# Eight weight chunks a step, loads ten chunks ahead, and small sums moved between engines in an attention and feed-forward kernel

## The chip, the cores and the metric

The kernel runs on one core of a Trainium2 chip. The metric is the device time of one execution in microseconds (us); where several runs were made, their median. Five engines work beside each other: TensorE (PE, with its weight loads as PEld), VectorE (DVE), ScalarE (ACT), GpSimd (POOL) and SyncE (SP), which issues all DMAs here. Each takes its instructions in the order in which they stand in its own stream, and they wait for each other by semaphores.

## The reference

Attention over 4 batches, 8 heads, 576 tokens and 64 dimensions, in which each query keeps only its 32 highest scores, then two feed-forward layers over the 2304 tokens:

```python
def _attn_ref(q, k, v):
    scores = scale * np.matmul(q, k.transpose(0, 1, 3, 2))
    kth = np.partition(scores, -top_k, axis=-1)[..., -top_k:-top_k + 1]
    mask = scores >= kth
    scores = np.where(mask, scores, -1000000000.0)
    scores = scores - np.max(scores, axis=-1, keepdims=True)
    attn = np.exp(scores)
    attn = attn / (np.sum(attn, axis=-1, keepdims=True) + 1e-09)
    return np.matmul(attn, v)

def _moe_ref(x, w_in, w_out, g_ln):       # 512 -> 1024 -> 512
    h = x @ w_in
    solu = h * softmax(h)
    ln = (solu - mu) / np.sqrt(var + 1e-06) * g_ln
    return ln @ w_out

def _moe2_ref(x, w_in, w_out):            # 512 -> 2048 -> 512
    h = x @ w_in
    g = h * (1.0 / (1.0 + np.exp(-1.702 * h)))
    return g @ w_out
```

(The softmax, the mean and the variance of the second function are shortened here.) Inputs and outputs are 32-bit.

## The kernel before

**Numbers.** Every matrix operand is split into a high and a low 16-bit half, and a product is made of three matmul passes. DVE, ACT and POOL make the halves: ACT writes the high one, POOL (or DVE) the difference. The weights come as 64-bit words: `w_load` brings a chunk of 128 x 1024 words (512 KB) into two slots of the tile `wt`, `w_decode` makes 32-bit numbers of it on DVE (two or three operations of 512 columns, L246 to L251, by way of a tile `wi` in PSUM), and `w_split` makes the two halves with ACT and POOL (L288, L135). There are 48 chunks: eight for w1, eight for w2, and four times four and four for the two matrices of the second layer.

**Attention** runs in 72 steps (18 blocks of queries, four or two steps in each). A step has `scores` (PE, L452), `copy_s` (ACT), `fold` and `rounds` (DVE, L470 to L484: the 32nd highest value by repeated maxima), `pick` (POOL, L494), `mask` (ACT and POOL, L502), `exp_of` (ACT), `high` and `low` (ACT and POOL, L520), `turn` (a transpose by DMA of `eh` into `et`, L525), and three steps later `back` (PE, L603: `av`). When a block's last step is back, `evac_main` or `evac_tail` divides by the sums of the exponentials: `recip` adds 1e-9 to the tile `rsum` and takes the reciprocal (L626, L627), once for each of the 20 blocks of queries (16 of 8 heads, 4 of half as many columns). The addition is two operations, on all columns but the last and on the last.

**Feed-forward** work comes in 18 blocks of 128 tokens, spread over 13 places of the program each, one place per step and two in steps 6 and 7 (`SLOTS`). Within it `c` is L804 (tile `h2`, shown as `h`), `gelu` L813, `g_low` L824 (tile `gh`) and `d` L831 (tile `o`). The buffers `t` and `y` are one pair (tag `t`), and `o` has one buffer, so that the next block's first `d` waits until `store` has made `y` of the last one.

**What sets the order.** The code is written in steps, and a scheduler then orders each engine's stream by its own estimate of times. `DECODE` says how many chunks are decoded in which step, `W_RAW` how many chunks ahead of the one being decoded are loaded, `W_STAGE` how many slots of `wt` must stay free when a load takes its two. After the first k and q tiles, `w_loads(-1)` starts the loads.

**The end.** `w_check` squares all weights on ACT (tile `junk`, sums into `insq`). At the end the sums of squares are added over the partitions (L1117, on POOL), several bounds are tested on DVE (`inside`, L1108 to L1111), the result `bad` is joined over the partitions (L1126, on POOL), and `flag` (L1128) decides on a branch to a second, exact version of the whole program, which does not run in the profiled execution.

Of the kernel before, what the change touches and what calls it, by code (L numbers as in the profile page):

```python
# [7 lines left out]
F32 = mybir.dt.float32  # L8
# [4 lines left out]
ALU = mybir.AluOpType  # L13
# [6 lines left out]
FIRST_RAW = (None, None, "h", "zt", None)  # L20
FIRST_HALF = (False, True, True, False, True)
W_RING = 4
W_RAW = 6
W_STAGE = 4
TWO_BANKS = 32
HP_W = 0
SIGNED = (1, 1, 0)
# [1 line left out]
DELAY = 0  # L29
HP_AT = 0  # L30
LAG = 3
DECODE = (4, 4, 4, 4, 8, 8, 8, 8)
SLOTS = {6: 2, 7: 2}
FIRST_SLOT = 6
R_BUFS = 2
# [5 lines left out]
TAIL_AT = (1,)  # L41
W_CHECK = 60
PIN_TO = -1
KV_BUFS, RAW_BUFS = 4, 2
S_IN = 2.0 ** 8
S_EXP = 2.0 ** -19
S_Z = 2.0 ** 10
# [4 lines left out]
def attn_moe_kernel(tc: tile.TileContext, *args):  # L52

    nc = tc.nc
    with ExitStack() as ctx:
        flag = layers(ctx, tc, True, *args)
        again = nc.values_load(flag, min_val=0, max_val=1)
    with tc.If(again > 0):
        with ExitStack() as ctx:
            layers(ctx, tc, False, *args)  # L60
# [19 lines left out]
def layers(ctx, tc, quick, q, k, v, w1, w2, g_ln, w3, w4, out):  # L80
# [5 lines left out]
    nc = tc.nc  # L86
    start = len(nc.cur_bb.bb.instructions)
# [10 lines left out]
    cst = ctx.enter_context(tc.tile_pool(name="cst", bufs=1))  # L98
# [6 lines left out]
    if quick:  # L105
        picks = cst.tile([128, B * S * H // 128, 3], F32, name="picks")
        pickc = cst.tile([128, 2, 3], F32, name="pickc")
        insq = cst.tile([128, 2 * B * NP + 24], F32, name="insq")
        qsq = cst.tile([128, B * (NEWT + 1)], F32, name="qsq")
        zsq = cst.tile([128, NBLK], F32, name="zsq")  # L110
        ysum = cst.tile([128, NBLK], F32, name="ysum")
        for i, x in enumerate((1.0, -S_EXP, BIG)):
            nc.vector.memset(pickc[:, :, i], x)

    lo_n = {}

# [31 lines left out]
    sm = ctx.enter_context(tc.tile_pool(name="sm", bufs=3))  # L148
    PS = bass.MemoryType.PSUM
    p_sc = ctx.enter_context(tc.tile_pool(name="p_sc", bufs=1, space=PS))  # L150
    p_av = ctx.enter_context(tc.tile_pool(name="p_av", bufs=1, space=PS))
# [43 lines left out]
    def room(i, n, keep):  # L195

        live = {r + z for r in at_raw.values() for z in range(2)}
        free = [r for r in range(i, WCH + SHIFT) if r not in live]
        fit = [r for r in free if all(r + z in free for z in range(n))
               and len(set(free) - {i, r, r + n - 1}) >= keep]  # L200
        if not fit:
            return None
        r = min(fit, key=lambda r: (max(used.get(r + z, -1) for z in range(n)), -r))
        for z in range(n):
            used[r + z] = i
        return r
# [415 lines left out]

    def recip(r, n):

        for a, b in ((0, n - 1), (n - 1, n)):
            nc.vector.tensor_scalar(r[:, a:b], r[:, a:b], 1e-9, None, op0=ALU.add)  # L626
        nc.vector.reciprocal(r, r)  # L627

    def evac_main(blk):
        b, r = blk  # L630
        if r == 0:
            batch_coef(b)
        recip(rsum[blk], 8)
        if quick:
            rr = rsum[blk].rearrange("p (a c) -> p a c", c=2)
        else:
            rr = sm.tile([128, 4, 2], F32, tag="rr", name="rr")
            iv = bsc[b][:, 1, 1, :]
            nc.vector.scalar_tensor_tensor(rr, rsum[blk].rearrange("p (a c) -> p a c", c=2), bcf[b][:, 1:2],
                                           iv[:, :, None].to_broadcast([128, 4, 2]), op0=ALU.mult, op1=ALU.mult)  # L640
        x = one.tile([128, 512], F32, tag="x", name="x")
        nc.vector.tensor_tensor(x.rearrange("p (h d) -> p h d", d=64),
                                pav[blk].rearrange("p (h d) -> p h d", d=64),
                                rr.rearrange("p a c -> p (a c)")[:, :, None].to_broadcast([128, 8, 64]),
                                op=ALU.mult)
        return x, None if quick else bcf[b][:, 2:3]
# [255 lines left out]
    def run(gen):  # L902
        for _ in gen:
            pass
# [49 lines left out]
    def w_loads(i, most=99):  # L954

        while wload[0] < min(WCH, i + 1 + W_RAW, most):
            j = wload[0]
            r = room(j, 2, max(1, min(W_STAGE, (WCH + SHIFT - j - 2) // 2)))
            if r is None:
# [6 lines left out]
    def decode(n):  # L966
        for _ in range(n):
            i = wnext[0]
            if i == WCH:
                return  # L970
            wnext[0] += 1
            with urgent(tc, HP_W):
                w_decode(i)
                w_split(i)
                w_loads(i)
# [47 lines left out]
    def place(name):  # L1023
        for f in slot.get(name, ()):
            with urgent(tc, HP_MOE):
                f()

    t = 0
    while True:
        count = 0 if t < FIRST_SLOT else SLOTS.get(t, 1)  # L1030
        live = t < NS
        for z in range(max(count, 1)):
# [53 lines left out]
            place("late")  # L1086
            if z < count - 1 and t < len(DECODE):
                decode(DECODE[t] // count)
        if live:
            for w in work.get(t, ()):  # L1090
                run(loaded.pop(0))
            if t < len(DECODE):
                decode(DECODE[t] - (DECODE[t] // max(count, 1)) * (max(count, 1) - 1))
        if W_CHECK <= t < W_CHECK + WCH // 2:
# [9 lines left out]
    ok = sm.tile([128, 6], F32, tag="ok", name="ok")  # L1104

    def inside(x, lo, hi, dst):

        nc.vector.tensor_scalar(junkc[:, 0:x.shape[1]], x, lo, None, op0=ALU.is_ge)  # L1108
        nc.vector.scalar_tensor_tensor(junkc[:, 0:x.shape[1]], x, hi, junkc[:, 0:x.shape[1]], op0=ALU.is_le,
                                       op1=ALU.mult)  # L1110
        nc.vector.tensor_reduce(dst, junkc[:, 0:x.shape[1]], axis=AX.X, op=ALU.min)  # L1111
# [1 line left out]
    short = one.tile([128, B * S * H // 128], F32, tag="zt", name="short")  # L1113
    nc.vector.scalar_tensor_tensor(short, picks[:, :, 2], -1.0 / BIG, picks[:, :, 0], op0=ALU.mult, op1=ALU.add)
    junkc = one.tile([128, short.shape[1]], F32, tag="x", name="junkc")
    tot = sm.tile([128, insq.shape[1]], F32, tag="tot", name="tot")
    nc.gpsimd.partition_all_reduce(tot, insq, channels=128, reduce_op=bass_isa.ReduceOp.add)  # L1117
    inside(tot, 4.0, 2.0 ** 15, ok[:, 0:1])
    inside(qsq, 2.0 ** -7, 2.0 ** 14, ok[:, 1:2])
    inside(short, -1e30, 0.0, ok[:, 2:3])  # L1120
    inside(zsq, 2.0 ** -28, 2.0 ** 60, ok[:, 3:4])
    inside(ysum, -1e30, 1e30, ok[:, 4:5])
    nc.vector.tensor_reduce(ok[:, 5:6], ok[:, 0:5], axis=AX.X, op=ALU.min)
    bad = sm.tile([128, 2], F32, tag="bad", name="bad")
    nc.vector.tensor_scalar(bad[:, 0:1], ok[:, 5:6], 0.5, None, op0=ALU.is_lt)
    nc.gpsimd.partition_all_reduce(bad[:, 1:2], bad[:, 0:1], channels=128, reduce_op=bass_isa.ReduceOp.max)  # L1126
    flag = sm.tile([128, 1], I32, tag="flag", name="flag")
    nc.vector.tensor_scalar(flag, bad[:, 1:2], 0.5, None, op0=ALU.is_gt)  # L1128
    return flag[0:1, 0:1]


# [28 lines left out]
```

## Time and profile before

| what | us |
|---|---|
| median of 3 runs | 978.17 (976.66 to 978.33) |
| the profiled execution | 977.06 |
| its span on the core | 975.3 |
| busy: PE, DVE, ACT, POOL | 761.6, 771.0, 721.1, 696.6 |
| granted TensorE clock, mean over the span | 0.929 of full speed |

The profiled execution lies 1.1 us under the median; 1.8 us of it lie outside the span. In the first 30 us the first tiles are loaded and turned. Up to some 260 us weights are loaded and decoded beside attention, until 840 us attention and feed-forward blocks run together, and what is left of the feed-forward blocks follows until 965 us. A row of the timeline gives start, duration, engine, line, operation, tiles (out<-in), shapes and, in brackets, how long the engine was idle before it and what ended that.

### The profile page before, as it was taken

How to read it: one execution, taken by the hardware profiler on the slowest of the kernel's cores; microseconds unless marked ns; L12 is line 12 of the kernel's file. 1: busy time of each engine (PE TensorE's matmuls, PEld its weight loads, DVE VectorE, ACT ScalarE, POOL GpSimd, SP SyncE). 2: the span in 40 equal slices, each digit the busy share in tenths (PEclk: the TensorE clock that was granted, in tenths of full speed). 3: DMA queues.
4: the chain of work that ended last, by engine and by line, in shares of the span. 5: the costliest groups of instructions: out<-in, count | busy, mean ns of one | idle time of the engine just before them, and what ended most of it. 6: DMA issues, size and time to landing. Idle time of an engine off the chain costs nothing.

```text
span 975.3 us, 22249 instructions
## 1 busy us (share of the span) xinstructions
PE 761.6 (78%) x8224; PEld 498.0 (51%) x8224; DVE 771.0 (79%) x2170; ACT 721.1 (74%) x1257; POOL 696.6 (71%) x700
## 2 busy tenths in 40 slices
PE   1123526546779899998979999898989999999975
PEld 0012213424446566665556766566565666666643
DVE  4999899989989889897798989889798899421210
ACT  4788888578888877878887877778887888743421
POOL 1489799688888887787878777687887677722311
PEclk9998667677999999999999999999989999999988
DMA  6998766476786756666856756668767555522100
GB/s 157 314 276 185 195 152 144 92 146 156 153 146 127 148 109 111 115 123 123 161 108 129 140 100 120 107 115 155 141 104 120 104 97 104 91 47 45 34 22 15
DMA packets 337733, 122.66 MB, mean 126 GB/s; under 512 B 315344, under 2 KB 329168, under 8 KB 337616
## 3 DMA queue, kind: packets, MB, share of 16 engines
q1 hardware_dynamic: 337616, 121.16, 60.5%
q8 instruction: 66, 1.08, 0.5%
q14 instruction: 51, 0.42, 0.1%
HBM read 39.85 MB, written 4.72 MB: 46 GB/s over the span
## 4 chain that ended last, share of the span: by engine, by line
POOL 21%; ACT 17%; PE 16%; DVE 15%; DMA 15%; issue 10%; SPq 5%; ACTq 0%; POOLq 0%; DVEq 0%
PE h L804 5%; POOL s L502 5%; PE o L831 5%; ACT s L157 5%; POOL eh L520 4%; DVE wk L481 4%; DVE wk L484 4%; DMA raw<-in_k_dram 3%; PE x L774 3%; POOL gh L824 2%; ACT r L157 2%; POOL e L768 2%; POOL wt L135 2%; POOL kq L135 2%; DMA vraw<-in_v_dram 2%
## 5 line engine op out<-in xcount | busy, mean ns | idle before, releaser
L481 DVE MAX8 wk<-wk 128x8 f32<-128x296 f32 x576 | 239.5, 453 | 0.0
L804 PE MATMUL h<-x2t,wt 128*128 128x128 f16 x3456 | 218.0, 225 | 23.4 <-DVE t L813 14.6
L804 PEld LDWEIGHTS <-wt 128*128 128x128 f16 x3456 | 207.4, 101 | 30.1 <-issue 13.4
L502 POOL TENSOR_TENSOR s<-s,r 128x576 f32<-128x576 f32 x144 | 181.6, 1281 | 43.0 <-ACT r L157 42.8
L520 POOL TENSOR_TENSOR eh<-s,eh 128x576 f16<-128x576 f32 x144 | 181.3, 1280 | 36.9 <-ACT eh L157 27.0
L831 PE MATMUL o<-wt,gh 128*128 128x512 f16 x864 | 201.3, 383 | 7.2 <-ACT y L157 7.1
L484 DVE MATCH_REPLACE8 wk<-wk 128x296 f32<-128x296 f32 x432 | 191.6, 449 | 0.0
L603 PE MATMUL av<-vt,et 128*128 128x64 f16 (+1 forms) x2400 | 90.9, 204 | 83.8 <-DMA et<-eh 78.8
L452 PE MATMUL sc<-kt,qt 128*128 128x64 f16 (+7 forms) x640 | 97.4, 320 | 63.3 <-DVE wk L473 45.6
L824 POOL TENSOR_TENSOR gh<-t,gh 128x512 f16<-128x512 f32 x72 | 83.4, 1159 | 80.5 <-ACT gh L157 73.5
L831 PEld LDWEIGHTS <-gh 128*128 128x128 f16 x864 | 83.9, 99 | 102.9 <-issue 11.3
L603 PEld LDWEIGHTS <-et 128*128 128x128 f16 (+1 forms) x2400 | 83.4, 108 | 97.6 <-DMA et<-eh 86.4
L157 ACT ACTIVATE s<-s,picks 128x576 f32<-128x576 f32 x144 | 110.1, 766 | 14.3 <-POOL s L502 14.0
L813 DVE SCALAR_TENSOR_TENSOR t<-t,h 128x512 f32<-128x512 f32 x72 | 48.6, 675 | 83.5 <-ACT t L157 81.5
L774 PE MATMUL x<-wt,zt 128*128 128x512 f16 x432 | 102.8, 392 | 14.8 <-DMA zt<-zh 13.2
L157 ACT ACTIVATE r<-s,picks 128x576 bf16<-128x576 f32 x144 | 103.2, 764 | 7.6 <-POOL picks L494 7.4
L707 PE MATMUL ha<-wt,xt 128*128 128x512 f16 x432 | 100.6, 391 | 10.3 <-DMA xt<-xhl 9.4
L452 PEld LDWEIGHTS <-qt 128*128 128x128 f16 (+1 forms) x640 | 48.8, 110 | 110.7 <-DVE wk L473 39.4
L157 ACT ACTIVATE s<-sc 128x1152 f32<-128x1152 f32 x72 | 80.4, 1117 | 17.8 <-PE sc L452 9.5
L157 ACT ACTIVATE wt<-wt 128x512 f16<-128x512 f32 (+1 forms) x115 | 68.5, 627 | 26.2 <-DVE wt L251 11.1
L157 ACT ACTIVATE t<-h 128x512 f32<-128x512 f32 x72 | 42.1, 584 | 59.9 <-PE h L804 54.8
L157 ACT ACTIVATE eh<-s 128x1152 f16<-128x1152 f32 x72 | 83.1, 1154 | 0.6
(81 smaller groups left out, 1066.1 us busy)
## 6 DMA issues: line engine op xcount, KB each, us to landing
wt<-in_moe_w_in_dram SPq DMA_DIRECT2D x24, 512.0 KB, 5.1
wt<-in_moe_w_out_dram SPq DMA_DIRECT2D x24, 512.0 KB, 6.1
qt<-qt SPq DMA_DIRECT2D x72, 64.0 KB, 2.0
raw<-in_k_dram SPq DMA_DIRECT2D x32, 128.0 KB, 2.7
raw<-in_q_dram SPq DMA_DIRECT2D x16, 256.0 KB, 3.2
vraw<-in_v_dram SPq DMA_DIRECT2D x32, 128.0 KB, 2.5
out_dram<-y SPq DMA_DIRECT2D x16, 256.0 KB, 2.4
et<-eh SPq DMA_TRANSPOSE x72, 4.7
```

The lines of the kernel that those rows point to most:

```text
L157: nc.scalar.activation(out, in_, func, **kw)
L452: nc.tensor.matmul(sc[rows, i * S + c0:i * S + c1], t[qi // 4][:, hl, qi % 4, rows], kts[kp][:, k0 + c0:k0 + c1], start=(hl == 0), stop=(h ...
L481: nc.vector.max(out=wk[:, i, at_:at_ + 8], in_=wk[:, i, 0:W_END])
L484: nc.vector.match_replace(out=wk[:, i, 0:W_END], in_to_replace=wk[:, i, at_:at_ + 8], in_values=wk[:, i, 0:W_END], imm_value=LOW)
L502: nc.gpsimd.tensor_tensor(s[:, i], s[:, i], r[i], op=ALU.subtract)
L520: nc.gpsimd.tensor_tensor(eh[:, 1, cols], s[:, i], eh[:, 0, cols], op=ALU.subtract)
L603: nc.tensor.matmul(o[rows, col:col + 64], et[:, ea, 4 * i + c, rows], vts[kp][:, va, vc:vc + 64], start=(n == 0), stop=(n == 14))
L707: nc.tensor.matmul(h[:, half * 512:half * 512 + 512], self.xt[:, a, kc], w1v(kc, w, half), start=(n == 0), stop=(n == 11))
L774: nc.tensor.matmul(self.x2, self.zt[:, a, kc], w2v(kc, w), start=(n == 0), stop=(n == 23))
L804: nc.tensor.matmul(h2[:, mm * 128:(mm + 1) * 128], w3v(kc, w, 4 * g + mm), self.x2t[:, a, kc], start=(n == 0), stop=(n == 11))
L824: nc.gpsimd.tensor_tensor(gh[:, 1], t.rearrange("p (a n) -> p a n", a=4), gh[:, 0], op=ALU.subtract)
L831: nc.tensor.matmul(self.o, gh[:, a, mm], w4v(4 * g + mm, w), start=(g == 0 and n == 0), stop=(g == 3 and n == 11))
```

## The change

Four edits:

- `DECODE` is (8, 8, 8, 8, 8, 8) in place of (4, 4, 4, 4, 8, 8, 8, 8), `W_RAW` 10 in place of 6, `W_STAGE` 6 in place of 4. The 48 chunks are asked for in steps 0 to 5 and loads run up to ten chunks ahead. `SLOTS` is as before.
- `recip` adds 1e-9 to all columns in one operation with two tensor inputs, (r + 1e-9) max r, in place of two operations with one.
- The sum of `insq` over the partitions is a matmul with a 128 x 128 tile of ones, into a PSUM tile that has the buffer of `av`, in place of POOL's partition sum.
- The joining of `bad` over the partitions is such a matmul too, of one column, and `flag` is read from PSUM. POOL sets the tile of ones to 1.0 at the start.

```diff
-W_RAW = 6
-W_STAGE = 4
+W_RAW = 10
+W_STAGE = 6
...
-DECODE = (4, 4, 4, 4, 8, 8, 8, 8)
+DECODE = (8, 8, 8, 8, 8, 8)
...
+        ones = cst.tile([128, 128], F32, name="ones")
+        nc.gpsimd.memset(ones, 1.0)
...
     def recip(r, n):
 
-        for a, b in ((0, n - 1), (n - 1, n)):
-            nc.vector.tensor_scalar(r[:, a:b], r[:, a:b], 1e-9, None, op0=ALU.add)
+        nc.vector.scalar_tensor_tensor(r[:, 0:n], r[:, 0:n], 1e-9, r[:, 0:n], op0=ALU.add, op1=ALU.max)
         nc.vector.reciprocal(r, r)
...
-    tot = sm.tile([128, insq.shape[1]], F32, tag="tot", name="tot")
-    nc.gpsimd.partition_all_reduce(tot, insq, channels=128, reduce_op=bass_isa.ReduceOp.add)
+    tot = p_av.tile([128, 512], F32, tag="av", name="tot")[:, 0:insq.shape[1]]
+    nc.tensor.matmul(tot, ones, insq, start=True, stop=True)
...
-    bad = sm.tile([128, 2], F32, tag="bad", name="bad")
-    nc.vector.tensor_scalar(bad[:, 0:1], ok[:, 5:6], 0.5, None, op0=ALU.is_lt)
-    nc.gpsimd.partition_all_reduce(bad[:, 1:2], bad[:, 0:1], channels=128, reduce_op=bass_isa.ReduceOp.max)
+    bad = sm.tile([128, 1], F32, tag="bad", name="bad")
+    nc.vector.tensor_scalar(bad, ok[:, 5:6], 0.5, None, op0=ALU.is_lt)
+    rows = p_av.tile([128, 512], F32, tag="av", name="rows")[:, 0:1]
+    nc.tensor.matmul(rows, ones, bad, start=True, stop=True)
     flag = sm.tile([128, 1], I32, tag="flag", name="flag")
-    nc.vector.tensor_scalar(flag, bad[:, 1:2], 0.5, None, op0=ALU.is_gt)
+    nc.vector.tensor_scalar(flag, rows, 0.5, None, op0=ALU.is_gt)
```

In the built programs the scheduler's order differs as well. Lines after the change are numbered two or three higher. First POOL's stream at the end of the program before, from the low half `gh` of the feed-forward blocks (the numbers tell the buffers of different stages apart; an ISA row is an instruction that belongs to the partition sum or to the change between it and other work):

```order
L824 TENSOR_TENSOR gh_13153<-t_13134,gh_13153 128x512
L1117 ISA
L1117 ISA tot_13463<-insq_75 128x56
L824 ISA
L824 TENSOR_TENSOR gh_13222<-t_13206,gh_13222 128x512
L824 TENSOR_TENSOR gh_13291<-t_13275,gh_13291 128x512
L824 TENSOR_TENSOR gh_13362<-t_13345,gh_13362 128x512
L824 TENSOR_TENSOR gh_13429<-t_13413,gh_13429 128x512
L1126 ISA
L1126 ISA bad_13481<-bad_13481 128x1
```

The same place after the change, from the same `gh` (now buffer 13135) to the load of the flag:

```order
L826 TENSOR_TENSOR gh_13135<-t_13116,gh_13135 128x512
L826 TENSOR_TENSOR gh_13204<-t_13188,gh_13204 128x512
L826 TENSOR_TENSOR gh_13273<-t_13257,gh_13273 128x512
L826 TENSOR_TENSOR gh_13344<-t_13327,gh_13344 128x512
L826 TENSOR_TENSOR gh_13411<-t_13395,gh_13411 128x512
L58 TENSOR_LOAD flag_13467
```

The two sums and the three other ISA rows are gone from POOL. On PE the matmul of `tot` stands behind the 48 `h` matmuls of the stage whose `gh` is 13273, ahead of the `o` matmuls that read `gh` 13204, and the matmul of `rows` is PE's last.

Second, SP's stream near the start, before: transposes of the third and fourth pair of heads' keys (`kt`), chunk loads (`wt`), the tail of q, the first v tiles and the first transposed exponentials (`et`):

```order
L356 DMA_TRANSPOSE kt<-kq 128x10x128
L215 DMA wt<-in_moe_w_in_dram 128x1024 x4
L391 DMA raw<-in_q_dram 64x2x64
L215 DMA wt<-in_moe_w_in_dram 128x1024
L356 DMA_TRANSPOSE kt<-kq 128x10x128
L215 DMA wt<-in_moe_w_in_dram 128x1024
L215 DMA wt<-in_moe_w_out_dram 128x1024 x2
L362 DMA vraw<-in_v_dram 128x256
...
L215 DMA wt<-in_moe_w_out_dram 128x1024 x6
L525 DMA_TRANSPOSE et<-eh 128x18x128
```

The same stretch of SP after the change:

```order
L359 DMA_TRANSPOSE kt<-kq 128x10x128
L218 DMA wt<-in_moe_w_in_dram 128x1024 x6
L218 DMA wt<-in_moe_w_out_dram 128x1024 x2
L394 DMA raw<-in_q_dram 64x2x64
L359 DMA_TRANSPOSE kt<-kq 128x10x128
L218 DMA wt<-in_moe_w_out_dram 128x1024 x6
L218 DMA wt<-in_moe_w_in_dram 128x1024 x2
L365 DMA vraw<-in_v_dram 128x256
...
L528 DMA_TRANSPOSE et<-eh 128x18x128
```

Sixteen chunk loads in place of eight stand ahead of the first v tile, and sixteen in place of fourteen ahead of the first `et`. On DVE the order of the decode differs little: the first 36 chunks' last operations (L251, now L254) stand behind the same number of folds as before, and the 48th stands behind the 17th fold in place of the 19th.

Third, DVE's stream at the second main block of queries, before (the reciprocal of `rsum` and what lies around it):

```order
L473 MAX wk<-sc 128x8 x2
L626 TENSOR_SCALAR rsum<-rsum 128x7
L246 TENSOR_SCALAR wi<-wt 128x512
L626 TENSOR_SCALAR rsum<-rsum 128x1
L481 MAX wk<-wk 128x8 x2
L251 SCALAR_TENSOR_TENSOR wt<-wt,wi 128x512
L627 RECIPROCAL rsum<-rsum 128x8
```

And after the change:

```order
L476 MAX wk<-sc 128x8 x2
L628 SCALAR_TENSOR_TENSOR rsum<-rsum 128x8
L253 SCALAR_TENSOR_TENSOR wi<-wt,wi 128x512
L484 MAX wk<-wk 128x8 x2
L629 RECIPROCAL rsum<-rsum 128x8
```

One operation stands where there were two, at the same place behind the fold's maxima.

## Rows read from the trace of the kernel before

**Rows 1.** The page's busy time, share of the span and instructions of each engine.

```profile
PE 761.6 (78%) x8224; PEld 498.0 (51%) x8224; DVE 771.0 (79%) x2170; ACT 721.1 (74%) x1257; POOL 696.6 (71%) x700
```

**Rows 2.** Busy time in three stretches; last: granted clock, DMA share, GB/s.

```profile
25.00:50.00 25.00, 4.18 (x16) 1.74 (x16) 24.05 (x63) 17.62 (x33) 12.64 (x16) 1.00 1.01 325
25.00:300.00 275.00, 135.62 (x1324) 85.28 (x1325) 259.77 (x675) 220.81 (x386) 228.64 (x226) 0.82 0.75 177
300.00:800.00 500.00, 466.76 (x5316) 309.93 (x5314) 439.50 (x1303) 405.56 (x704) 395.50 (x400) 0.98 0.66 122
```

**Rows 3.** Timeline near the end, 935 to 957 us, the rows around PE's gap.

```profile
935.80 0.62 ACT L157 ACTIVATE gh<-t 128x512 f16<-128x512 f32 x1
936.59 2.84 PE L804 MATMUL h<-x2t,wt 128*128 128x128 f16 x48
936.93 0.68 POOL L1117 PARTITION_ALL_REDUCE tot<-insq  x1 [5.85 <-ACT gh L157]
...
939.53 0.60 ACT L157 ACTIVATE t<-h 128x512 f32<-128x512 f32 x1 [3.12 <-PE h L804]
...
944.59 1.14 POOL L824 TENSOR_TENSOR gh<-t,gh 128x512 f16<-128x512 f32 x1 [6.98 <-issue]
945.76 0.60 ACT L157 ACTIVATE y<-o 128x512 f32<-128x512 f32 x1 [5.63 <-POOL gh L824]
...
946.50 4.65 PE L831 MATMUL o<-wt,gh 128*128 128x512 f16 x12 [7.07 <-ACT y L157]
...
953.67 2.75 PE L831 MATMUL o<-wt,gh 128*128 128x512 f16 x12
```

**Rows 4.** The stretch of those slower matmuls, with columns as in rows 2.

```profile
946.50:951.00 4.50, 4.50 (x13) 1.66 (x13) 0.00 (x0) 0.47 (x1) 1.15 (x1) 0.57 0.15 58
```

**Rows 5.** Timeline of PE behind a shorter wait in the same stage.

```profile
913.00 3.63 PE L774 MATMUL x<-wt,zt 128*128 128x512 f16 x16 [1.58 <-DMA zt<-zh]
```

**Rows 6.** Timeline of the last two instructions.

```profile
968.21 0.38 POOL L1126 PARTITION_ALL_REDUCE bad<-bad  x1 [5.80 <-issue]
968.62 0.15 DVE L1128 TENSOR_SCALAR flag<-bad 128x1 int32<-128x1 f32 x1 [2.55 <-POOL bad L1126]
```

**Rows 7.** DVE's groups by shape: xcount | busy us, mean ns | idle before.

```profile
L626 DVE TENSOR_SCALAR rsum<-rsum 128x7 f32<-128x7 f32 x16 | 15.3, 958 | 4.1 <-ACT s L157 4.1
L250 DVE SCALAR_TENSOR_TENSOR wi<-wt,wi 128x512 int32<-128x512 int32 x21 | 14.3, 681 | 0.0
...
L627 DVE RECIPROCAL rsum<-rsum 128x8 f32<-128x8 f32 x16 | 3.0, 190 | 0.1
...
L626 DVE TENSOR_SCALAR rsum<-rsum 128x1 f32<-128x1 f32 x20 | 2.8, 140 | 4.7 <-ACT s L157 4.7
```

**Rows 8.** Timeline of the longest addition on DVE and of POOL beside it.

```profile
170.36 9.36 DVE L626 TENSOR_SCALAR rsum<-rsum 128x7 f32<-128x7 f32 x1
...
170.27 1.17 POOL L135 TENSOR_TENSOR wt<-wt 128x512 f16<-128x512 f32 x1
...
178.53 1.17 POOL L135 TENSOR_TENSOR wt<-wt 128x512 f16<-128x512 f32 x1
```

**Rows 9.** Timeline of another addition on DVE and of POOL beside it.

```profile
721.45 0.63 DVE L626 TENSOR_SCALAR rsum<-rsum 128x3 f32<-128x3 f32 x1 [0.38 <-ACT s L157]
...
720.89 1.16 POOL L824 TENSOR_TENSOR gh<-t,gh 128x512 f16<-128x512 f32 x1
```

**Rows 10.** Timeline of DVE and POOL near 14 us, and all of L288 (ns min/median/max).

```profile
13.83 0.83 DVE L138 SCALAR_TENSOR_TENSOR kq<-raw,kq 128x640 f16<-128x640 f32 x1 [0.94 <-ACT kq L157]
...
14.40 1.27 POOL L288 TENSOR_TENSOR wt<-wt 128x512 f32<-128x512 f32 x1 [0.92 <-ACT wt L157]
...
L288 POOL TENSOR_TENSOR wt<-wt x27: 1144/1156/1272, 12.3 to 249.2; 128x512 f32<-128x512 f32 x27
```

**Rows 11.** Timeline of ACT: the first v tile, and the fifth step's score copy.

```profile
44.17 0.74 ACT L157 ACTIVATE vraw<-vraw 128x640 f32<-128x640 f32 x1 [0.41 <-DMA vraw<-in_v_dram]
...
64.56 1.10 ACT L157 ACTIVATE s<-sc 128x1152 f32<-128x1152 f32 x1
```

More of the change, by code (lines that the diff above doesn't have):

```diff
@@ L43 @@
 PIN_TO = -1
-KV_BUFS, RAW_BUFS = 4, 2
+KV_BUFS = 4
+RAW_BUFS = 2
 S_IN = 2.0 ** 8
```

## The prediction

> **What bounds the kernel now.** I read the busy shares first, then the windows by stage, then the stretch in which the matmul engine drains, then single lines. No engine is the bound of the whole run: PE 78%, DVE 79%, ACT 74%, POOL 71% of the span [rows 1]. By stage it differs. From 25 to 300 us, where weight chunks are decoded beside attention, DVE is busy 259.8 of 275 us (94%) and PE 136. From 300 to 800 us PE is busy 466.8 of 500 and DVE 439.5 [rows 2]. After some 840 us attention is over, only the feed-forward blocks drain, and PE is their bound. So a microsecond of DVE is worth most before 300 us, and after 840 us each idle stretch of PE is a loss.
>
> Such a stretch is there. PE ends the h matmuls that began at 936.59 at 939.43 (2.84 us) and starts the next o matmul at 946.50: 7.07 us idle. Followed back: o waits for ACT's y (945.76), y for POOL's gh (944.59), because y takes the buffer of t that this gh reads. Its ACT half was ready at 936.42 (935.80 + 0.62), yet POOL began it 6.98 us after the sum over partitions had ended, waiting for nothing that the profile shows [rows 3]. The order of before has a row "ISA" ahead of the sum and another ahead of that gh; I read the 6.98 us as the second one. The idle time costs twice: the granted clock was 0.57 in 946.5 to 951, and the 12 matmuls there took 4.65 us, against 2.75 for the next twelve [rows 3, 4].
>
> **The drain (gain 7.5 us).** The first sum becomes one PE matmul, and POOL runs its gh rows without anything between. This gh can then run at 936.5 and end at 937.7. ACT's order is still t, y, gh, so y starts when t ends, 939.53 + 0.60 = 940.13, and o starts 0.74 us later, as it did before (945.76 to 946.50): 940.87 in place of 946.50, a gain of 5.63 us. PE then idles some 1.4 us in place of 7.1. After the 1.58 us wait at 913.00 sixteen matmuls took 3.63 us, 0.23 each, as in the next twelve (2.75 / 12) [rows 5], so I take the clock as kept: 4.65 - 2.75 = 1.90 us more. What is late next is y behind ACT's t; it leaves the 1.4 us. The new matmul, 56 columns of 32-bit data, is queued on PE just ahead of that o group and waits for ACT's last check of the weights, which stands ahead of the gh of 935.80 on ACT and is over by then. No row shows a 32-bit matmul. Nearest rows: 48 of 128 columns in 2.84 us (0.06 each) and 12 of 512 in 2.75 (0.23 each); as an estimate 0.1 to 1.6 us, from two of the short to seven of the long. Up to 1.4 us it lies inside the idle time and costs nothing; above that it moves o by 0.2. DVE's checks of it stand ahead of one gelu row, whose reader has 2.6 us of o matmuls to spare.
>
> **The last sum (gain 1.9 us).** DVE's flag waited 2.55 us, from the end of bad on DVE to 968.62, and the sum on POOL began 5.80 us after POOL's last gh, not after bad [rows 6]. In its place stands a matmul of one column: 0.1 to 1.6 us by the same rows. I take 0.6, since one column is nearer to the short one: 2.55 - 0.65 = 1.9 us, bounds 0.9 to 2.4. All of it is on the path. The 6.5 us from the flag to the end of the span stay.
>
> **The small additions (gain 1.7 and 4 us).** Each of the 20 calls of recip loses one DVE operation: 20 x 0.140 = 2.8 us [rows 7]. DVE is the bound for part of the run only, so I count 0.6 of that, 1.7 us (0 to 2.8). The other one changes its kind, and that is the larger matter. The addition on 7 columns takes 0.958 us in the mean, though it has less to do than the reciprocal on 8 (0.190): the 16 of 7 columns make 15.3 us [rows 7]. One alone took 9.36 us, from 170.36 to 179.72; POOL ran without a gap all that time and ended at 179.70 [rows 8]. Another began at 721.45 during a POOL operation and ended with it, at 722.08 against 722.05 [rows 9]. So this addition waits for POOL: mostly for the operation that is running, once for a whole string of them. Does the two-tensor form wait as well? The rows of two-tensor operations with one input in PSUM do not stretch beside a busy POOL (L250: 21 with a mean of 681 ns) [rows 7]. But the new form reads two inputs, both in SBUF. Only one of that kind met POOL: L138 ran from 13.83 to 14.66, and the POOL operation that began at 14.40 took 1.27 us, the longest of 27 (median 1.156) [rows 10]. I go by that nearest row: they still exclude each other. Then the other fifteen stay (15.3 - 9.36 = 5.9 us, 0.40 in the mean). For the long one I take a wait for the running operation, as in those: some 1.2 us, a gain of 8.1 us of DVE. DVE is the bound there, but later steps catch up with part, so I count half: 4 us. Bounds: all 12.9 us above the 0.15 of an undisturbed one (16 x 0.15 = 2.4) saved, or a long string met again (0).
>
> The Trainium skill speaks against this edit: its page "SBUF — State Buffer", section "Who interferes with whom", says that a VectorE instruction with two SBUF inputs contends with a GpSimd instruction that reads SBUF, and that the later one is held until the first finishes. The stretched POOL operation agrees with it; that a wait outlasts a whole string, as the 9.36 us did, it does not say. By the rule the sum stays as above; without it the second rival below holds.
>
> **The decode and its loads (0, bounds -3 to +5 us).** The table asks for eight chunks a step from step 0, but what the scheduler makes of it is nearly the old order: on DVE the first 36 chunks finish behind the same number of folds as before, and the 48th behind the 17th fold in place of the 19th. DVE's work is the same and it was busy 94% there, so I count nothing. The loads do move: eight more of 512 KB stand ahead of the first v loads on SP, and two more ahead of the first et transpose. At the 325 GB/s of the first stretch [rows 2] eight take some 13 us. ACT needed the first v at 44.17 and had waited 0.41 for it; now it lands near 57, and ACT's order has its reader behind the second step's exponentials, at about that time. The cover ends at the score copy of 64.56: PE's order now has one av matmul, which needs v and et, inside the score matmuls ahead of it [rows 11]. With ACT's copies (0.74 us the first) behind the landing these end near 62, some 2 us early. If that cover is gone, up to 5 us are lost. On the other side DVE is idle 15 us in 25 to 300, of which loads that come earlier could give back 3.
>
> **Sum.** 7.5 + 1.9 + 1.7 + 4 = 15.1 us. The profiled execution took 977.06, so 962.0. The median of the runs is 978.17, 1.1 above it, so the forecast for the median is 963.
>
> **Rivals** (times on the same footing).
> 1. The additions meet a long string again: the decode phase keeps POOL full (228.6 of 275 us busy [rows 2]), and the same 9 us are lost in another call. Then the 4 us are missing: 967.
> 2. The two-tensor form does not wait for POOL at all. For: the rows with one input in PSUM; against: the stretched operation [rows 10]. Then about two thirds of 12.9 us come back, 8.6 in place of 4: 958.
> 3. Slower: strings of POOL work catch more of the first three calls, all in the decode phase. Two more strings of 9 us, where DVE is the bound and little is made up: 978.2 - 11.1 + 18 = 985. With one more it is 976, so it decides from the second on. For it: POOL's share; against: one string in sixteen additions.
> 4. The change does less than it says in the drain: the 32-bit matmul is at its upper bound and the clock falls in spite of the shorter idle time (1.9 + 1 us), and the loads cost their 5: 971.
>
> **How the numbers follow.** The forecast has 0.45, rivals 1 to 4 have 0.15, 0.2, 0.08 and 0.12. The forecast's own range is 958 to 970. For 8 in 10, the lower end is rival 2 with the loads' 3 us and the rest of the second operation's 1.1 (954, rounded down to 953) and the upper one rival 4 with the rest of its bounds (975). A measurement tells about 0.2% (2 us) from no change: faster is below 976.2. Faster takes nearly all of the forecast, of rivals 1 and 2 and most of rival 4: 0.87; the same 0.05; slower 0.08.
>
> **What would show it.** In the profile after: no idle time over 2 us of PE between the h and o groups near the end, with a granted clock near 1.00 there; flag within 1 us of bad; some 20 additions on DVE whose mean is 0.3 to 0.6 us beside POOL (0.15 would be rival 2, one of over 5 us rival 1); attention over some 6 us earlier than now. What would make the forecast wrong: a step in 60 to 300 us that waits for et or v, or a shorter PE idle time that does not arrive at the end.

## The result and the profile after

The changed kernel takes 961.85 us (median of 5 runs, 961.29 to 967.89), the kernel before 978.17: a ratio of 0.9857, 95% interval 0.9827 to 0.9887. (Ratios and intervals are estimated from all runs and not from the two medians, whose quotient is 0.983 here; in the experiments the two differ by 0.0013 at most.) The profiled execution, 967.89 us, is the longest of the five, so the rows below account for 9.2 of the some 16 us between the medians.

The page's busy line and the same stretches as in [rows 1, 2] (busy us of PE, PEld, DVE, ACT, POOL, instructions in brackets; granted clock, DMA share, GB/s):

```profile
PE 766.2 (79%) x8228; PEld 497.6 (52%) x8228; DVE 766.7 (79%) x2150; ACT 722.9 (75%) x1257; POOL 695.9 (72%) x699
```

```profile
25.00:300.00 275.00, 139.79 (x1350) 86.28 (x1351) 254.68 (x662) 218.83 (x382) 226.47 (x225) 0.76 0.72 176
300.00:800.00 500.00, 470.11 (x5332) 309.38 (x5331) 442.95 (x1309) 412.63 (x713) 400.05 (x405) 0.98 0.68 123
```

In the first stretch DVE gets through fewer instructions than before (662 against 675), in the second through a few more. Nothing here looks like a gain of 1.4%. What this execution gained is plain at the end. The timeline (start, duration, engine, line, tiles, idle time before and its releaser), where [rows 3, 4, 6] showed the two gaps:

```profile
936.00 0.62 ACT L160 ACTIVATE gh<-t 128x512 f16<-128x512 f32 x1
936.69 1.16 POOL L826 TENSOR_TENSOR gh<-t,gh 128x512 f16<-128x512 f32 x1 [5.41 <-ACT gh L160]
936.79 2.84 PE L806 MATMUL h<-x2t,wt 128*128 128x128 f16 x48
939.48 0.38 PE L1119 MATMUL tot<-insq,ones 128*128 128x56 f32 x2
939.74 0.60 ACT L160 ACTIVATE t<-h 128x512 f32<-128x512 f32 x1 [3.12 <-PE h L806]
940.23 0.59 ACT L160 ACTIVATE y<-o 128x512 f32<-128x512 f32 x1
...
940.96 2.75 PE L833 MATMUL o<-wt,gh 128*128 128x512 f16 x12 [1.11 <-ACT y L160]
```

```profile
958.49 0.15 DVE L1127 TENSOR_SCALAR bad<-ok 128x1 f32<-128x1 f32 x1
958.69 0.30 PEld L1129 LDWEIGHTS rows<-bad,ones 128*128 128x128 f32 x2 [2.34 <-DVE bad L1127]
958.69 0.38 PE L1129 MATMUL rows<-bad,ones 128*128 128x1 f32 x2 [1.85 <-DVE bad L1127]
959.11 0.16 DVE L1131 TENSOR_SCALAR flag<-rows 128x1 int32<-128x1 f32 x1 [0.47 <-PE rows L1129]
```

POOL's `gh` follows its ACT half at once, PE idles 1.11 us in place of 7.07, and the twelve `o` matmuls behind take 2.75 us in place of 4.65, at a granted clock of 1.00 where it was 0.57 [rows 4]. Columns as in [rows 2], over these twelve:

```profile
940.96:943.71 2.75, 2.75 (x15) 1.32 (x15) 2.54 (x8) 0.63 (x1) 1.16 (x1) 1.00 0.25 95
```

From the start of the 48 `h` matmuls to `flag` it is 22.3 us (936.79 to 959.11), before 32.0 (936.59 to 968.62): 9.7 us.

The addition does not fare as hoped. All 20 (minimum/median/maximum in ns, first and last start), then the longest on DVE, then POOL beside it:

```profile
L628 DVE SCALAR_TENSOR_TENSOR rsum<-rsum x20: 148/162/8205, 87.2 to 841.1; 128x8 f32<-128x8 f32 x16, 128x4 f32<-128x4 f32 x4
```

```profile
169.37 8.21 DVE L628 SCALAR_TENSOR_TENSOR rsum<-rsum 128x8 f32<-128x8 f32 x1
177.50 0.68 DVE L253 SCALAR_TENSOR_TENSOR wi<-wt,wi 128x512 int32<-128x512 int32 x1
```

```profile
169.22 1.16 POOL L291 TENSOR_TENSOR wt<-wt 128x512 f32<-128x512 f32 x1
170.33 2.53 POOL L523 TENSOR_TENSOR eh<-s,eh 128x576 f16<-128x576 f32 x2
172.80 1.17 POOL L138 TENSOR_TENSOR wt<-wt 128x512 f16<-128x512 f32 x1
173.91 2.53 POOL L505 TENSOR_TENSOR s<-s,r 128x576 f32<-128x576 f32 x2
176.38 1.17 POOL L138 TENSOR_TENSOR wt<-wt 128x512 f16<-128x512 f32 x1
```

The new form waits through seven POOL operations (some rows hold two), at the place at which the old one waited through eight [rows 8]. The additions take 13.9 us of DVE in all, in place of 20.2.

### The profile page after: what moved, and what is told of

Same layout as the page of the kernel before. It is cut to its first block, busy times and chain, and to the rows that moved or that the text cites. A ratio compares the mean times of both kernels' runs of the same rounds, so it can differ in the third digit from the quotient of the medians.

```text
span 966.0 us, 22236 instructions
## 1 busy us (share of the span) xinstructions
PE 766.2 (79%) x8228; PEld 497.6 (52%) x8228; DVE 766.7 (79%) x2150; ACT 722.9 (75%) x1257; POOL 695.9 (72%) x699
## 4 chain that ended last, share of the span: by engine, by line
PE 26%; ACT 16%; DVE 16%; DMA 15%; POOL 14%; issue 8%; SPq 4%; ACTq 0%; POOLq 0%; DVEq 0%
PE h L806 9%; PE o L833 7%; ACT s L160 4%; PE x L776 4%; DVE wk L484 4%; POOL eh L523 4%; DVE wk L487 4%; PE ha L709 3%; POOL s L505 3%; POOL wt L138 2%; PE sc L455 2%; DMA kt<-kq 2%; ACT kq L160 2%; DMA qt<-kq 2%; DMA et<-eh 2%
## 5 line engine op out<-in xcount | busy, mean ns | idle before, releaser
L484 DVE MAX8 wk<-wk 128x8 f32<-128x296 f32 x576 | 242.2, 461 | 0.0
L487 DVE MATCH_REPLACE8 wk<-wk 128x296 f32<-128x296 f32 x432 | 193.6, 458 | 0.0
L455 PE MATMUL sc<-kt,qt 128*128 128x64 f16 (+7 forms) x640 | 99.3, 321 | 71.7 <-DMA qt<-kq 30.8
L776 PE MATMUL x<-wt,zt 128*128 128x512 f16 x432 | 105.4, 397 | 14.3 <-DMA zt<-zh 14.2
L160 ACT ACTIVATE wt<-wt 128x512 f16<-128x512 f32 (+1 forms) x115 | 68.0, 627 | 22.9 <-DVE wt L254 10.5
```

The lines of the kernel that those rows point to most:

```text
L160: nc.scalar.activation(out, in_, func, **kw)
L455: nc.tensor.matmul(sc[rows, i * S + c0:i * S + c1], t[qi // 4][:, hl, qi % 4, rows], kts[kp][:, k0 + c0:k0 + c1], start=(hl == 0), stop=(h ...
L484: nc.vector.max(out=wk[:, i, at_:at_ + 8], in_=wk[:, i, 0:W_END])
L487: nc.vector.match_replace(out=wk[:, i, 0:W_END], in_to_replace=wk[:, i, at_:at_ + 8], in_values=wk[:, i, 0:W_END], imm_value=LOW)
L776: nc.tensor.matmul(self.x2, self.zt[:, a, kc], w2v(kc, w), start=(n == 0), stop=(n == 23))
```

## The experiments

Each kernel ran beside the kernel before on the same chip. "us" is (ratio - 1) x 978.2.

| kernel | ratio to before | 95% interval | us |
|---|---|---|---|
| changed, a second time | 0.9826 | 0.9806 to 0.9845 | -17.0 |
| both sums alone | 0.9881 | 0.9862 to 0.9901 | -11.6 |
| table alone | 0.9901 | 0.9884 to 0.9919 | -9.7 |
| new addition alone | 1.0068 | 1.0052 to 1.0084 | +6.7 |
| changed, old additions | 0.9781 | 0.9758 to 0.9805 | -21.4 |
| changed, old table | 0.9982 | 0.9962 to 1.0001 | -1.8 |
| changed, reduction for addition | 0.9758 | 0.9733 to 0.9783 | -23.7 |
| changed, no addition | 0.9685 | 0.9660 to 0.9710 | -30.8 |
| changed, sums in pairs | 0.9833 | 0.9807 to 0.9859 | -16.3 |
| addition alone, as reduction | 1.0020 | 0.9997 to 1.0042 | +2.0 |
| before, rsum strided | 0.9989 | 0.9966 to 1.0011 | -1.1 |
| W_RAW and W_STAGE alone | 0.9926 | 0.9898 to 0.9955 | -7.2 |

The three parts alone make -11.6 - 9.7 + 6.7 = -14.6 us, between the two measurements of the whole (-14.0 and -17.0). Up to the end the changed kernel with the old additions has the order of the table alone on every engine, and the one with the old table that of the new addition alone; the parts add up to -21.3 and -4.9 us there, measured were -21.4 and -1.8. In the experiments the theory was the prediction's (the sums gain 9.4, the addition 5.7, the table 0); the first rival, that the gain of the additions is missing; the second, that the order of the instructions carries the difference.

**The changed kernel once more**

> The changed kernel once more, unaltered. In its first profile one addition still waited 8.2 us behind a string of POOL work, and that execution took 967.9 us where the other four took 961.3 to 963.6. If the string is met by chance and explains the spread, this profile has either no addition above 2 us and a time near 962, or one of about 8 us and a time near 968. If the string is met in every execution, an addition of about 8 us stands here too, at a time near 962, and the 6 us lie elsewhere.

Median 961.4 us of 7 runs (960.5 to 966.21); this profiled execution took 965.35 and has an addition of 8.05 us at 169.44. The changed kernel with the old table has one of 8.79 us, the one with the old additions one of 8.21, the addition alone one of 8.78, the table alone one of 8.23. Each comes near 170 us. So the long wait is not the chance of one execution. Of the two readings the second holds as to the addition; but this profiled execution, too, is 4 us over its median, and why stays open.

**The changed kernel without the addition, with the old additions, with the old table**

```diff
-        nc.vector.scalar_tensor_tensor(r[:, 0:n], r[:, 0:n], 1e-9, r[:, 0:n], op0=ALU.add, op1=ALU.max)
         nc.vector.reciprocal(r, r)
```

> The changed kernel without the addition of 1e-9 ahead of the reciprocal (left out altogether: no two-tensor operation, nothing that could wait for POOL). Theory: the two-tensor addition still waits for POOL (13.9 us of DVE in the profile after, of which one wait of 8.2), and half of it arrives at the end: 4 to 7 us less than the changed kernel, near 956. Rival: the waits lie beside other work and cost nothing: within 1.5 us of the changed kernel.

Ratio 0.9685, 948.45 us: the fastest of all, 13 us under the changed kernel, more than the theory's 7. But compared place by place, the additions aside, some 650 of DVE's 1682 instructions are others than in the changed kernel, so it does not tell the wait from the order.

```diff
-        nc.vector.scalar_tensor_tensor(r[:, 0:n], r[:, 0:n], 1e-9, r[:, 0:n], op0=ALU.add, op1=ALU.max)
+        for a, b in ((0, n - 1), (n - 1, n)):
+            nc.vector.tensor_scalar(r[:, a:b], r[:, a:b], 1e-9, None, op0=ALU.add)
```

> The changed kernel with the two old additions (seven columns and one) in place of the two-tensor one. The prediction counts 1.7 us for the second operation and 4 for the string: 5.7 us slower than the changed kernel. If the form of the addition is indifferent, because both wait for POOL alike, only the second operation's 1.7 us remain, or nothing.

Ratio 0.9781: not 5.7 us slower than the changed kernel but 4.4 to 7.4 faster, although its additions take 20.4 us of DVE against 13.9. Both readings fail; the two-tensor addition, with the order that comes with it, is a loss here.

```diff
-W_RAW = 10
-W_STAGE = 6
+W_RAW = 6
+W_STAGE = 4
...
-DECODE = (8, 8, 8, 8, 8, 8)
+DECODE = (4, 4, 4, 4, 8, 8, 8, 8)
```

> The changed kernel with the old decode table, 6 buffers of raw weights and 4 staged. The prediction counts 0 for the table (bounds: a gain of 3 us to a loss of 5), so within 1.5 us of the changed kernel. Rival: the new order and the earlier loads are worth what the additions were thought to bring; then this is 4 to 7 us slower than the changed kernel, and the one with the old additions is not.

Ratio 0.9982: with the old table 12 to 15 us of the gain are gone. The prediction's 0 fails. The rival is right in both signs (slower with the old table, not slower with the old additions), but its 4 to 7 us are less than half of what the table is worth here.

**Each part alone**

Each is a piece of the change's diff, put into the kernel before. The sums:

```diff
+    nc.tensor.matmul(tot, ones, insq, start=True, stop=True)
...
+    nc.tensor.matmul(rows, ones, bad, start=True, stop=True)
```

> The kernel before with both sums over the partitions on PE, and nothing else of the change. Every engine's order is that of the kernel before up to the last feed-forward blocks, so this measures the end alone. Theory: 7.5 + 1.9 = 9.4 us less, near 968.8, ratio 0.990. The changed kernel with the old table took 976.3, only 2 us under the kernel before, though it has both sums: if the sums bring 9.4, its new additions (with the order that comes with them) cost 7.5 us rather than gain 5.7. Rival: the sums bring under 3 us, because something else than PE sets the end, and the new additions are neutral.

Ratio 0.9881, -11.6 us (9.7 to 13.5): a little more than the 9.4. All engines keep the old order up to the end, and the trace shows the same 9.7 us there: 22.3 from the `h` matmuls (938.20) to `flag` (960.51).

The addition:

```diff
+        nc.vector.scalar_tensor_tensor(r[:, 0:n], r[:, 0:n], 1e-9, r[:, 0:n], op0=ALU.add, op1=ALU.max)
```

> The kernel before with the two-tensor addition alone. The prediction counts a gain of 5.7 us (972.5). Theory now, from the two undo experiments: the two-tensor addition with the order that the scheduler makes of it is a loss of some 5 to 7.5 us, so 983 to 986. Rival: the addition is neutral by itself and it is only bad together with the new table, so within 1.5 us of the kernel before.

Ratio 1.0068, +6.7 us: slower by itself, as the undo experiment said. The loss lies in 180 to 320 us, behind the long wait. Busy times there of the kernel before, then of this one, then what DVE waited for most, in the kernel before and in this one (us in total, times, longest):

```profile
180.00:320.00 140.00, 99.17 (x999) 64.01 (x997) 129.31 (x373) 114.02 (x201) 115.21 (x116) 0.87 0.69 138
```

```profile
180.00:320.00 140.00, 101.04 (x1006) 64.45 (x1004) 121.46 (x346) 113.55 (x201) 113.29 (x115) 0.85 0.69 139
```

```profile
DVE st L712 <- PE ha L707: 2.8, 1, 2.8
DVE wk L470 <- ACT s L157: 2.2, 3, 1.5
```

```profile
DVE wk L470 <- ACT s L157: 6.0, 4, 3.2
DVE t L812 <- ACT t L157: 3.9, 1, 3.9
DVE wi L246 <- DMA wt<-in_moe_w_in_dram: 2.4, 1, 2.4
DVE wi L246 <- DMA wt<-in_moe_w_out_dram: 1.8, 1, 1.8
```

DVE idles 18.5 of 140 us in place of 10.7: 7.9 more, for score copies, for `t`, and for weight loads that its new order asks for earlier than they land.

The table:

```diff
+W_RAW = 10
+W_STAGE = 6
...
+DECODE = (8, 8, 8, 8, 8, 8)
```

> The kernel before with the new decode table, W_RAW and W_STAGE alone. The prediction counts 0 (bounds -3 to +5 us). Theory now: the table, by the order that it brings, gives 12 to 15 us (the changed kernel with the old table was 15 us slower; with the old additions the changed kernel took 956.0, 12.8 under 968.8), so near 964. Rival: the 15 us need the new additions as well (the two change the same order): within 3 us of the kernel before.

Ratio 0.9901, -9.7 us, somewhat short of the 12 to 15 that it is worth in the changed kernel. The rival's bound of 3 us is passed as well. The gain does not lie where the table acts: in 25 to 300 us DVE is busy 260.7 us, before 259.8. It comes after the decode is over: of POOL's 72 selections (`picks`) the 25th starts 1.6 us earlier than before (336.4), the 49th 9.8 us (586.3) and the last 9.4 us (827.4). Two stretches, before and then with the table:

```profile
300.00:420.00 120.00, 113.03 (x1329) 74.81 (x1327) 108.33 (x324) 97.12 (x168) 95.81 (x98) 0.99 0.63 120
420.00:560.00 140.00, 128.73 (x1477) 85.93 (x1476) 121.14 (x362) 114.06 (x201) 112.66 (x117) 0.98 0.68 131
```

```profile
300.00:420.00 120.00, 109.48 (x1312) 72.48 (x1310) 111.66 (x331) 96.84 (x167) 95.66 (x93) 1.00 0.67 119
420.00:560.00 140.00, 132.65 (x1558) 87.67 (x1555) 124.88 (x374) 118.53 (x209) 116.10 (x119) 1.00 0.72 135
```

DVE idles 30.5 of these 260 us before and 23.5 with the table. What it waited for there (300 to 560), first before, then with the table:

```profile
DVE wk L470 <- ACT s L157: 10.8, 10, 4.1
DVE st L724 <- ACT e L157: 10.6, 5, 3.1
DVE t L813 <- ACT t L157: 3.4, 2, 1.7
DVE rsum L626 <- ACT s L157: 3.1, 2, 2.0
```

```profile
DVE st L724 <- ACT e L157: 8.2, 6, 3.0
DVE wk L470 <- ACT s L157: 8.0, 6, 3.7
...
DVE t L813 <- ACT t L157: 0.4, 1, 0.4
```

The same kinds of waits for ACT are shorter or gone. The decode's own instructions are as many as before; compared place by place, some 750 of DVE's 1722 and some 580 of ACT's 985 instructions are others, most of DVE's attention and feed-forward work. That these moves make the gain, and not the deeper buffers, is argued and not shown.

Of the table only the first two lines:

```diff
+W_RAW = 10
+W_STAGE = 6
```

> The kernel before with W_RAW 10 and W_STAGE 6, and the old DECODE table. The three together gave 8.6 us (ratio 0.990). Theory 1: loads that run further ahead are what helps: ratio 0.988 to 0.993 here. Theory 2: the decode in steps 0 to 5 helps, and the loads are idle without it: 0.998 to 1.002. Theory 3: neither by itself; what counts is the order that the scheduler happens to make, which is another one here: then the ratio may lie anywhere from 0.985 to 1.01, and the first 300 us, where loads and decode are, show no gain of that size.

Ratio 0.9926, -7.2 us, within theory 1's range. But its cause is not shown to be the loads: of the kernels whose addition has a form that waits, this is the only one without the long wait. Its 40 additions:

```profile
L626 DVE TENSOR_SCALAR rsum<-rsum x40: 127/154/1422, 82.9 to 836.6; 128x1 f32<-128x1 f32 x20, 128x7 f32<-128x7 f32 x16, 128x3 f32<-128x3 f32 x4
```

The addition that waited 9.36 us now starts at 171.95 beside an idle POOL. They take 12.0 us together, 8.2 less than before, so a missed string and earlier loads can't be told apart by the ratio. The trace speaks for neither alone: the 13th selection on POOL starts 6.2 us earlier than before (199.75), the 28th 11.6 us later (373.95), the 46th at the same time (559.4) and the last 6.0 us earlier (830.8). What was won by the missed string is lost again by 374 us, and what arrives at the end is won after 559, where no chunk is loaded or decoded. That is nearest to theory 3, the order. Where `DECODE` alone would come out was not run.

**The wait at a fixed order**

```diff
-        nc.vector.scalar_tensor_tensor(r[:, 0:n], r[:, 0:n], 1e-9, r[:, 0:n], op0=ALU.add, op1=ALU.max)
+        nc.vector.tensor_reduce(r[:, 0:n], r[:, 0:n][:, :, None], axis=AX.X, op=ALU.max)
```

> The changed kernel with each two-tensor addition replaced by a reduction over an axis of length one, which leaves the sums as they are (so the addition of 1e-9 is left out) and reads one input. All five engines keep the changed kernel's order exactly; only these 20 operations differ. So this is the price of the waits for POOL with the order held fixed. Theory A, the waits are what leaving out the addition gave: 8 to 13 us less than the changed kernel, 948 to 953. Theory B, the wait of 8 us costs about half, as the prediction counted: 4 to 5 us less, near 957; the rest of the 13 us is the other order. Theory C, the order alone: within 1 us of the changed kernel. If the reduction waits for POOL as well, its mean stays near 0.7 us and nothing is told apart.

Ratio 0.9758. The reduction never waits:

```profile
L628 DVE TENSOR_REDUCE rsum<-rsum x20: 129/146/162, 87.6 to 828.1; 128x8 f32<-128x8 f32 x16, 128x4 f32<-128x4 f32 x4
```

At the place of the long addition, with the same full POOL beside it (first DVE's row, then POOL's), it takes 0.13 us, so what the addition waited for was no input of its own:

```profile
169.96 0.13 DVE L628 TENSOR_REDUCE rsum<-rsum 128x8 f32<-128x8 f32 x1
```

```profile
169.83 1.18 POOL L291 TENSOR_TENSOR wt<-wt 128x512 f32<-128x512 f32 x1
170.95 2.54 POOL L523 TENSOR_TENSOR eh<-s,eh 128x576 f16<-128x576 f32 x2
```

With every other instruction at its place, 10.5 to 11 us less of DVE time made the kernel 6.7 to 9.7 us faster (against 0.9826 and 0.9857): between theories A and B, and most of the wait arrives at the end.

The same line in the kernel with the addition alone:

> The kernel before with the addition replaced by a reduction over an axis of length one (one input, does not wait for POOL; the addition of 1e-9 is left out). All engines keep the order of the kernel with the two-tensor addition alone, which took 984.3 (ratio 1.0068). Theory: that kernel was slower than before, although its additions took 14.3 us of DVE in place of 20.2, because of the order that the scheduler makes with one operation less; without the waits (11.4 us of DVE) it falls by 7 to 9 us to 975 to 977, ratio 0.998 to 1.000, and that is the same order's loss of 7 to 9 us against the kernel before without waits. Rival: the two-tensor form's waits alone made it slower; then it falls to about 966 (ratio 0.989 or less).

Ratio 1.0020: of the 6.7 us of loss 4.7 go with the waits (11.3 us of DVE, 14.3 to 3.0), 2.0 stay; the interval, 0.9997 to 1.0042, just reaches 1. The theory's 0.998 to 1.000 is missed by little, the rival's 0.989 clearly. In this order the same wait is worth less than half. And with 17 us less of DVE's time than the kernel before (3.0 us of additions for 20.2) it is still not faster. DVE, busy 117.7 of the 140 us in 180 to 320 against 129.3, waits more there: this order loses what the operations gain.

```diff
-            rsum[blk] = sm.tile([128, 8], F32, tag="rsum", name="rsum")
+            rsum[blk] = sm.tile([128, 8, 2], F32, tag="rsum", name="rsum")[:, :, 0]
```

The tail blocks' tile is changed in the same way.

> The kernel before with the tile rsum laid out two elements apart (a column used, a column not), and nothing else: all computation is kept, and all five engines have the order of the kernel before exactly. A one-input operation of one column never waited for POOL in the kernel before, one of seven neighbouring columns did. Theory 1: what waits is the form with neighbouring columns, so the additions fall from 20.2 us to some 6 us, the wait of 9.4 us with them; at a fixed order the changed kernel gained 8 us from the loss of its 8.2, so some 8 us less than before, ratio 0.991 to 0.993. Theory 2: any seven columns of an SBUF-to-SBUF operation wait; the additions stay near 20 us and the time at that of before.

Theory 2, ratio 0.9989, and the long addition is as it was:

```profile
170.64 9.38 DVE L626 TENSOR_SCALAR rsum<-rsum 128x7 f32<-128x7 f32 x1
```

**The addition kept, as a reduction over pairs**

```diff
+        ring.append(cst.tile([128, 8, 2], F32, tag=f"rs{i}", name="rsum"))
+        nc.gpsimd.memset(ring[i][:, :, 1], 1e-9)
...
-        nc.vector.scalar_tensor_tensor(r[:, 0:n], r[:, 0:n], 1e-9, r[:, 0:n], op0=ALU.add, op1=ALU.max)
...
+        r = rsum[blk] = sm.tile([128, 8], F32, tag="rsum", name="rsum")
+        nc.vector.tensor_reduce(r[:, 0:n], pair[blk][:, 0:n, :], axis=AX.X, op=ALU.add)
```

> The changed kernel with the addition kept but in a form that should not wait for POOL: the sums stand in a tile with 1e-9 beside each of them, and a reduction over these pairs (one input, like the one that was held up nowhere) adds the two. All computation is kept. The operation is estimated a little differently, so the scheduler makes another order than that of the changed kernel. Theory: the additions fall from some 13.5 us to under 4 us and none is above 0.3 us; without the waits the changed kernel's order gave a ratio of 0.976 and the order without any addition 0.969, so 0.967 to 0.978 here, faster than the changed kernel (0.983). Rival: the order decides as much as the wait does; then this one may fall outside, at 0.98 or above, although no addition waits.

The text on record is wrong in one point: in the blocks of half as many columns this kernel multiplies by the sums and not by their reciprocals. The operations are the same in number and kind, so its time can be read, though in these four blocks the multiplication need not wait for the reciprocal.

Ratio 0.9833, the rival. No addition waits (the longest of 20 is 0.17 us), as in the kernel with the other reduction, and yet the two are 7.3 us apart. The reduction reads 16 columns in place of 8, the sums stand in tiles of their own, three memsets come at the start, and with that, place by place, some 640 of DVE's 1702 instructions are others than in the changed kernel. Which of these edits the scheduler answers to was not tried. Where it falls behind, first this kernel, then the one with the other reduction:

```profile
500.00:520.00 20.00, 16.46 (x159) 9.96 (x156) 14.67 (x43) 14.63 (x29) 15.56 (x14) 0.91 0.87 169
520.00:540.00 20.00, 20.00 (x296) 13.69 (x294) 15.95 (x50) 18.00 (x29) 16.19 (x17) 1.00 0.49 98
```

```profile
500.00:520.00 20.00, 19.86 (x161) 10.96 (x159) 18.67 (x57) 18.46 (x32) 17.94 (x18) 1.00 0.88 169
520.00:540.00 20.00, 18.09 (x300) 13.07 (x299) 19.96 (x62) 17.91 (x32) 16.79 (x19) 1.00 0.58 108
```

DVE is busy 30.6 of 40 us against 38.6; its waits in 490 to 560 are all for ACT and PE, the longest 2.4 us.

## Why the prediction was right, and where its steps were not

963 was forecast and 961.85 measured. The number came out by luck: one term of the sum holds; of the others one has the wrong sign (12.4 us off) and one is missing (9.7 us), and these two happen to cancel nearly.

**The drain and the last sum: right, in each term.** In the trace `o` starts 4.17 us after the `h` matmuls' start in place of 9.91 (5.7 us; 5.63 in the prediction), the clock gives 1.90 (1.90), and `flag` waits 0.47 us in place of 2.55 (2.1; 1.9). Together 9.7 us against 9.4; the run with the sums alone gives 11.6 with an interval that begins at 9.7 (10.4 by the medians). The 32-bit matmul, put at 0.1 to 1.6 us, is two records of 0.27 us that end 0.38 after the first began, and it lies inside the idle time. The stretch of POOL that no row explained went with the partition sum and its ISA rows: without them `gh` follows 0.07 us after its ACT half. That it was the second of these rows, as the prediction reads it, fits and is not shown. Rival 4 fails.

**The small additions: +5.7 us of gain forecast, a loss of 6.7 measured.** Two steps failed. First, that the long wait shrinks to one running operation, some 1.2 us, had as its only ground that one string was met in sixteen additions; it measured 8.21. It is rival 1: the addition near 170 us comes at the same place in the order, beside a POOL that is full, and a string holds it there in eight of the nine kernels traced whose addition has a form that waits (the changed kernel counted once; the one with W_RAW and W_STAGE alone is the ninth). The second failed step has no term at all: the prediction looked at one place in DVE's order, saw one operation where two had stood, and took the rest of the order as given. With one operation less the scheduler orders everything behind it anew, and that order leaves DVE idle 7.9 us more in 180 to 320. Rival 3 expected a loss, but from further strings, and there is none: besides the long one no addition in any kernel traced takes over 1.5 us. That half of a DVE microsecond arrives at the end was too little in one order (0.6 to 0.9) and about right in the other (0.4).

**Rival 2** fails: the two-tensor form waits. The rule of the Trainium skill (page "SBUF — State Buffer", section "Who interferes with whom"), by which a VectorE instruction with two SBUF inputs contends with a GpSimd instruction that reads SBUF, is borne out: the five longest additions of the changed kernel end within 0.03 us of a POOL operation's end. The same section says that a reduction never contends on this chip; the 60 reductions that stand in for additions here, 0.17 us at most, agree.

**Decode and loads: 0 forecast, 9.7 us gained (12 to 15 in the changed kernel).** The step that failed is "nearly the old order". It compared how many folds stand ahead of each chunk's last operation, which indeed hardly changed, and left out what else moved. The bounds, -3 to +5, came from loads and DVE's idle time before 300 us. There the reading was good: the first v copy on ACT moved from 44.17 to 55.43, and the fifth step's score copy started at 64.65 in place of 64.56, so the cover held. The gain lies between 300 and 560 us, where DVE idles 7 us less, mostly in waits for ACT; the term that was put at nothing measures 9.7. Which of the moved instructions does it was not settled.

**What it looked for.** No idle time of PE over 2 us near the end, a clock of 1.00, `flag` within 1 us of `bad`: all seen. Additions of 0.3 to 0.6 us in the mean: not seen, they take 0.70, and the one of 8.21 us is the sign that the prediction gave for rival 1. Attention over 6 us earlier: the profiled execution shows 2.0 (the last selection on POOL starts at 834.76 in place of 836.73). That execution is 6 us over its median, and where the other executions save these 6 us no trace shows.

## What to carry to other kernels

Where a scheduler orders the streams by estimated times, an edit is two edits: the operations, and the order that comes with them. Here two programs with the same twenty reductions, none of which waits, differ by 7 us, as much as a wait of 8 us on the busiest engine costs; beside small edits only their order sets them apart. So the order of the whole stream belongs in a prediction, at least as a term of some 7 us with either sign; and a change made of parts is worth keeping in parts, since this one without its new addition is 4 to 7 us faster.

To price a wait, replace the waiting operation by one that the scheduler puts at the same place, and compare the orders first.

## What the runs showed of the hardware

A short DVE operation can be held by POOL much longer than one operation, and not always when POOL is full. At 527.47 us of the changed kernel an addition on four columns, first DVE's row, then POOL's:

```profile
527.47 0.95 DVE L628 SCALAR_TENSOR_TENSOR rsum<-rsum 128x4 f32<-128x4 f32 x1
```

```profile
527.12 2.52 POOL L505 TENSOR_TENSOR s<-s,r 128x576 f32<-128x576 f32 x2 [1.67 <-ACT r L160]
```

The row holds two POOL operations that follow each other without a gap. The addition was over at their seam (the first ends at 528.40, the addition at 528.42), while the one at 169.37 was not over at any of six such seams. What tells the two apart stays open.

Not only two-input forms wait: near the end a check with one input, 128 x 144, took 1.19 us from 941.91, while POOL's `gh` ran from 941.86 to 943.02; in the kernel before, with POOL idle, it took 0.23. In the six kernels traced that add to one column by itself, none of these 120 additions took over 0.16 us. Seven columns take 0.96 us in the mean in the kernel before, and 0.99 with the columns two elements apart: spreading them does not help.
